# A decode attention and gated-MLP kernel: an eleventh load buffer, the output projection in pieces among the last V products, and a two-pass variance

## The chip, the cores and the metric

The kernel runs on one core of one Trainium2 chip. The metric is the device time of the program in microseconds, slower or faster by the median of its runs.

## The reference

Two branches read the same input `x` (4 tokens of 1024) and are mixed by a gate.

```python
g = sigmoid((x * gate_w).sum(-1, keepdims=True))
# branch A: attention of one new token over a cache, B=4, H=32, Sk=8192, Dh=128
q = x @ wq                                   # 1024 x 4096
p = softmax(q . k_cache * Dh**-0.5)          # k_cache, v_cache: 4 x 32 x 8192 x 128 bf16
a = (p @ v_cache).reshape(B, 1, 4096) @ wo   # 4096 x 1024
# branch B: gated MLP, F = 3584
z = gelu(x @ w_in); z1, z2 = halves of z
z2 = (z2 - mean) / sqrt(var + eps)
b = (z1 * (w_sp * z2 + b_sp)) @ w_out
out = g * a + (1 - g) * b
```

The caches are 2 x 128 tiles of 2 MB (one per token and head). With the weights the kernel reads 564.7 MB, and each byte of the cache is used once.

## The kernel before

All loads go through a ring of `NSLOT` slots of 2 MB, issued in one fixed order by SyncE. A load waits until its slot's last reader on TensorE is done.

```python
NSLOT = 10
LAG = 40                     # V of head t-40 is used at step t
...
BW_AT = [4 + (i * (LAG - 8)) // max(1, nbw) for i in range(nbw)]   # steps 4..30: 4 w_in, 2 w_out tiles
WO_AT = [NK + LAG - 18 + 2 * k for k in range(H // 8)]             # 4 w_o tiles, 18 V tiles before the end
for t in range(NK + LAG):    # the order of the loads
    # t == 0: 4 w_q tiles;  t < 128: one K tile;  BW_AT: one w_in/w_out tile
    # WO_AT: one w_o tile as eight DMAs of 256 KB;  t >= 40: one V tile
    ...
```

At step `t` TensorE transposes K tile `t` (64 matmuls against the identity, evacuated by VectorE and ScalarE), then computes the scores of tile `t-1` and so frees its slot, then the V product of tile `t-40`. The first w_in tile is not used before step 41:

```python
def task_zT(t):
    ...
    if not dma_planned(r) or t < LAG + 1 or t < item_step[r] + 2:
        return False
```

After the 32 heads of a token their scores go through a softmax. Scores of the next token wait for it (`exp_done`), because they use the same PSUM banks. In that time TensorE may transpose two more K tiles, but frees no slot.

The layer norm of branch B takes mean and mean of squares in one pass (one matmul with ones for both). The output projection comes last:

```python
# after the last V product
d_ot = event("dve")
plan("dve", lambda E: E.tensor_copy(OT_sb[:, 0:Bn * 32], PS[:, OT_OFF:OT_OFF + Bn * 32]), waits=[last_pv], ev=d_ot)
for qi, r in enumerate(wo_items):
    def fn_a(E, qi=qi, s=s):
        for hh in range(8):
            for c in range(NC_):          # 4 x 8 x 8 = 256 matmuls, 4 columns each
                ins = E.matmul(PS[:, AT_OFF + c * Bn:...], lhsT=ring[:, s, hh * DM + c * 128:...], rhs=otv[:, h, :], ...)
    plan("pe", fn_a, waits=waits, ev=p_a)
# then: diff, times gate, plus B; 8 transposes; copy; output DMA
```

Of the kernel before, what the change touches and what calls it, by code (L numbers as in the profile page):

```python
# [5 lines left out]
BF = mybir.dt.bfloat16  # L6
# [2 lines left out]
ALU = mybir.AluOpType  # L9
AX = mybir.AxisListType  # L10

NSLOT = 10
SLOT_COLS = 8192
LAG = 40
KT_BANKS = (4, 5, 7)
# [5 lines left out]
def bass_gated_mix__mha_block_cached__mixer_gmlp__decode_kernel(  # L21
# [41 lines left out]
    RMAXT_OFF = 3584  # L63
    GMB_OFF = 3712
    SUM_OFF = 3713
    XTB_OFF = 5 * 1024

    es = ExitStack()
    with es:
# [9 lines left out]
        Q4 = sbt("Q4", [128, 128], F32)  # L79
        onesF = sbt("onesF", [128, 128], F32)  # L80
        IrowB = sbt("IrowB", [128, 1024], BF)
        x_sb = sbt("x_sb", [128, DM], BF)
        gw_sb = sbt("gw_sb", [128, DM], BF)
        xT_sb = sbt("xT_sb", [128, NI * Bn], BF)
        Qm = sbt("Qm", [128, Bn * H * 32], BF)
        zwork = sbt("zwork", [128, 6, NZ], F32)
# [7 lines left out]
        E2_sb = sbt("E2_sb", [128, 2, 2048], BF)  # L94
        OT_sb = sbt("OT_sb", [128, 128], BF)
        out_sb = sbt("out_sb", [128, DM], BF)
        junk = sbt("junk", [128, DM], BF)
        sm = sbt("sm", [128, 16], F32)
        wspb = sbt("wspb", [128, 2], BF)
        gm_sb = sbt("gm_sb", [128, 160], F32)  # L100
# [110 lines left out]
        item_step = {}  # L211
        nbw = len(extra) - 4
        BW_AT = [4 + (i * (LAG - 8)) // max(1, nbw) for i in range(nbw)]
        WO_AT = [NK + LAG - 18 + 2 * k for k in range(H // 8)]
        for t in range(NK + LAG):
            if t == 0:
                for q in range(4):
# [165 lines left out]
        gel = zwork[:, 4, :]  # L383
        z2sq = zwork[:, 5, 0:NFH * Bn]
        gT = zwork[:, 1, 0:NFH * Bn]
        bstate = dict(z_next=0, z_done=None, d8=None, bt_done=False, ln_planned=False, d6=None, d6a=None)

        def task_zT(t):
            q = bstate["z_next"]
# [27 lines left out]
        def plan_bchain(z_done):  # L417
            d1 = event("dve")
            plan("dve", lambda E: E.tensor_copy(zz, PS[:, ZT_OFF:ZT_OFF + NZ]), waits=[z_done], ev=d1)
            add_reader(6, d1)  # L420
            d2 = event("dve")
            plan("dve", lambda E: E.tensor_tensor(zsq, zz, zz, ALU.mult), waits=[d1], ev=d2)
            d3 = event("dve")
            plan("dve", lambda E: E.tensor_scalar(zsq, zsq, 0.044715, 1.0, op0=ALU.mult, op1=ALU.add),
                 waits=[d2], ev=d3)
            d4 = event("dve")
            plan("dve", lambda E: E.tensor_tensor(targ, zsq, zz, ALU.mult), waits=[d3], ev=d4)
            a_sg = event("act")
            plan("act", lambda E: E.activation(sg, targ, ACTF.Sigmoid, scale=GELU_C2), waits=[d4], ev=a_sg)
            d5 = event("dve")  # L430
            plan("dve", lambda E: E.tensor_tensor(gel, zz, sg, ALU.mult), waits=[a_sg], ev=d5)
            z2v = gel[:, NFH * Bn:NFC * Bn]
            d6a = event("dve")
            plan("dve", lambda E: E.tensor_reduce(st[:, 0:Bn], z2v.rearrange("p (f b) -> p b f", b=Bn), AX.X, ALU.add),
                 waits=[d5], ev=d6a)
            d6b = event("dve")
            plan("dve", lambda E: E.tensor_tensor(z2sq, z2v, z2v, ALU.mult), waits=[d5], ev=d6b)
            d6 = event("dve")
            plan("dve", lambda E: E.tensor_reduce(st[:, Bn:2 * Bn], z2sq.rearrange("p (f b) -> p b f", b=Bn),
                                                  AX.X, ALU.add), waits=[d6b], ev=d6)  # L440
            bstate["d6"] = d6
            bstate["d6a"] = d6a
            bstate["d4"] = d4

        def task_LN(t):
            if bstate["ln_planned"] or bstate["d6"] is None:
                return False
            bstate["ln_planned"] = True
            p_ln = event("pe")
            plan("pe", lambda E: E.matmul(PS[:, LN_OFF:LN_OFF + 2 * Bn], lhsT=onesF[:, :], rhs=st[:, 0:2 * Bn],  # L450
                                          start=True, stop=True),
                 waits=[bstate["d6"], bstate["d6a"], g_ones] + readers(6), ev=p_ln)
            d7a = event("dve")
            plan("dve", lambda E: E.tensor_scalar(st[:, 8:8 + 2 * Bn], PS[:, LN_OFF:LN_OFF + 2 * Bn], 1.0 / FH, None,
                                                  op0=ALU.mult), waits=[p_ln], ev=d7a)
            add_reader(6, d7a)
            mean = st[:, 8:8 + Bn]
            ex2 = st[:, 8 + Bn:8 + 2 * Bn]
            d7b = event("dve")
            plan("dve", lambda E: E.tensor_tensor(st[:, 24:24 + Bn], mean, mean, ALU.mult), waits=[d7a], ev=d7b)  # L460
            d7 = event("dve")
            plan("dve", lambda E: E.tensor_tensor(st[:, 16:16 + Bn], ex2, st[:, 24:24 + Bn], ALU.subtract),
                 waits=[d7b], ev=d7)
            a_std = event("act")
            plan("act", lambda E: E.activation(st[:, 20:20 + Bn], st[:, 16:16 + Bn], ACTF.Sqrt, bias=sm[:, 7:8],  # L465
                                               scale=1.0), waits=[d7, g_sm], ev=a_std)
            d_rstd = event("dve")
            plan("dve", lambda E: E.reciprocal(st[:, 28:28 + Bn], st[:, 20:20 + Bn]), waits=[a_std], ev=d_rstd)
            z2v = gel[:, NFH * Bn:NFC * Bn]
            z2m = z2v.rearrange("p (f b) -> p f b", b=Bn)  # L470
            gTm = gT.rearrange("p (f b) -> p f b", b=Bn)
            dg = None
            for b in range(Bn):
                dg = event("dve")
                plan("dve", lambda E, b=b: E.tensor_scalar(gTm[:, :, b], z2m[:, :, b], st[:, 8 + b:9 + b],
                                                           st[:, 28 + b:29 + b], op0=ALU.subtract, op1=ALU.mult),
                     waits=[d_rstd, bstate["d4"]], ev=dg)
            dg2 = event("dve")
            plan("dve", lambda E: E.tensor_scalar(gT, gT, sm[:, 8:9], sm[:, 9:10], op0=ALU.mult, op1=ALU.add),
                 waits=[dg, d_wsp], ev=dg2)  # L480
            d8 = event("dve")
            z1v = gel[:, 0:NFH * Bn]
            plan("dve", lambda E: E.tensor_tensor(uT[:, :], z1v, gT, ALU.mult), waits=[dg2], ev=d8)
            bstate["d8"] = d8
            return True
# [114 lines left out]
        def softmax_stage(b):  # L600
# [29 lines left out]
            elif st_ == 1:  # L630
# [14 lines left out]
                e2_ready[b] = e5  # L645
                sm_state[b] = 2

        def plan_PV(b, h):
            nonlocal last_pv
            r = kv_items[("V", b, h)]  # L650
            wt = need(r)
            s = slot_of(r)
            pv_ev = event("pe")

            def fn_v(E, s=s, b=b, h=h):
                ins = None
                col = OT_OFF + b * 32 + h
                for j in range(JT):
                    ins = E.matmul(PS[:, col:col + 1], lhsT=ring[:, s, j * 128:(j + 1) * 128],  # L659
                                   rhs=E2_sb[:, b % 2, j * 32 + h:j * 32 + h + 1], start=(j == 0), stop=(j == JT - 1))  # L660
                return ins
            waits = [wt] + readers(6)
            if h == 0:
                waits += [e2_ready[b], qstate["qm_ready"]]
            plan("pe", fn_v, waits=waits, ev=pv_ev)
            consume(r, pv_ev)
            last_pv = pv_ev
            return pv_ev

        pendS = []  # L670
        pv_next = 0
        t = 0
        while pv_next < NK:
            newT = None
            if t == 0:
                task_QT(t)
# [29 lines left out]
        assert bstate["bt_done"]  # L706
        exp_done_last = exp_done[Bn - 1]

        d_ot = event("dve")
        plan("dve", lambda E: E.tensor_copy(OT_sb[:, 0:Bn * 32], PS[:, OT_OFF:OT_OFF + Bn * 32]), waits=[last_pv], ev=d_ot)  # L710
        add_reader(6, d_ot)
        otv = OT_sb[:, 0:Bn * 32].rearrange("p (b h) -> p h b", h=32)
        p_a = None
        for qi, r in enumerate(wo_items):
            wt = need(r)
            s = slot_of(r)
            p_a = event("pe")

            def fn_a(E, qi=qi, s=s):
                ins = None  # L720
                for hh in range(8):
                    h = qi * 8 + hh
                    for c in range(NC_):
                        ins = E.matmul(PS[:, AT_OFF + c * Bn:AT_OFF + (c + 1) * Bn],  # L724
                                       lhsT=ring[:, s, hh * DM + c * 128:hh * DM + (c + 1) * 128],
                                       rhs=otv[:, h, :],
                                       start=(h == 0 and c == 0), stop=(h == H - 1 and c == NC_ - 1))
                return ins
            waits = [wt]
            if qi == 0:  # L730
                waits += [d_ot] + readers(6)
            plan("pe", fn_a, waits=waits, ev=p_a)
        for r in wo_items:
            consume(r, p_a)
        assert next_dma == len(items)
# [2 lines left out]
        prod = fin[:, 1, 0:NCB]  # L738
        outT = fin[:, 2, 0:NCB]
        d_f1 = event("dve")  # L740
        plan("dve", lambda E: E.tensor_tensor(diff, PS[:, AT_OFF:AT_OFF + NCB], BT_sb[:, 0:NCB], ALU.subtract),
             waits=[p_a, bstate["d_bt"]], ev=d_f1)
        d_f2 = event("dve")
        plan("dve", lambda E: E.tensor_tensor(prod.rearrange("p (c b) -> p c b", b=Bn),
# [65 lines left out]
```

## Time and profile before

| | before |
|---|---|
| median of the runs | 1390.78 us (15 runs, 1388.83 to 1394.03) |
| span of the profiled run | 1386.9 us (a run of 1388.73 us) |
| HBM read | 564.7 MB |
| 2 MB tile in the V stage | every 4.90 us |
| start of the last V product to the end | 14.96 us |

From the page of the kernel before, the span in 40 slices of 34.7 us: DMA busy share in tenths, and the rate in GB/s.

```profile
DMA  9999997999999999999999999999999999998994
GB/s 353 420 419 420 416 417 306 383 417 427 424 424 426 425 425 427 426 424 426 425 425 425 427 426 425 426 426 425 425 426 426 423 428 425 425 380 352 414 427 183
```

The DMA engines are the limit: 9 tenths and about 425 GB/s in all but a few slices. The Trainium skill ("DMA: Bandwidth & Descriptors", Specifications) states a fabric ceiling of 435 GB/s, and the trace saturates 2% below it. So one reads this profile by its holes: the first slice, the slice of 306 (208 to 243 us), those of 380 and 352, and the last.

The end of the timeline (start us, duration us, engine, line of the kernel, operation; in brackets the idle time before it and what ended it). PE is TensorE and PEld its weight loads, DVE is VectorE, ACT ScalarE, POOL GpSimd, and SPq the queue of SyncE:

```profile
1371.94 1.86 PE L659 MATMUL PS<-E_sb,ring 128*128 128x1 bf16 x64 [3.00 <-DMA ring<-in_A_v_cache_dram]
1373.84 0.29 DVE L710 CAST OT_sb<-PS 128x128 bf16<-128x128 f32 x1 [207.64 <-PE PS L659]
...
1374.28 6.97 PE L724 MATMUL PS<-OT_sb,ring 128*128 128x4 bf16 x256 [0.48 <-DVE OT_sb L710]
1381.29 0.19 DVE L741 TENSOR_TENSOR fin<-PS,BT_sb 128x32 f32<-128x32 f32 x1 [7.15 <-PE PS L724]
...
1381.99 1.87 PE L755 MATMUL PS<-identF,fin 128*4 128x128 f32 x8 [0.74 <-DVE fin L749]
...
1385.13 0.29 SPq L761 DMA_DIRECT2D out_dram<-out_sb  x1
```

When the last V tile has landed, nothing is left to stream, and 15 us of dependent work follow, 7 us of them the projection.

The first softmax, in windows of 3 us (window, length, then busy time and instruction count of PE, PEld, DVE, ACT and POOL, then granted clock, DMA share and GB/s):

```profile
221.00:224.00 3.00, 3.00 (x42) 2.90 (x43) 1.97 (x4) 1.02 (x1) 0.00 (x0) 0.69 0.56 240
224.00:227.00 3.00, 3.00 (x70) 2.78 (x70) 1.65 (x3) 1.99 (x2) 0.00 (x0) 1.00 0.68 191
227.00:230.00 3.00, 3.00 (x70) 2.67 (x67) 2.35 (x5) 2.11 (x3) 0.00 (x0) 1.00 0.92 377
...
233.00:236.00 3.00, 1.89 (x31) 1.53 (x27) 2.06 (x4) 2.35 (x3) 0.00 (x0) 1.00 1.00 399
236.00:239.00 3.00, 2.38 (x40) 2.36 (x40) 1.86 (x5) 2.75 (x2) 0.00 (x0) 1.00 0.38 164
239.00:242.00 3.00, 1.86 (x31) 1.51 (x27) 1.86 (x4) 2.31 (x5) 0.00 (x0) 1.00 0.02 5
242.00:245.00 3.00, 2.11 (x66) 1.92 (x66) 1.83 (x4) 0.84 (x1) 0.00 (x0) 1.00 0.00 0
245.00:248.00 3.00, 2.78 (x54) 2.55 (x47) 3.00 (x4) 1.12 (x2) 0.00 (x0) 1.00 0.95 284
```

The last column falls to 240 and 191, recovers, and then goes to 164, 5 and 0. Lost stream is the sum of (425 - rate)/425 x 3 us: 3.3 us in 221-230, 8.8 us in 236-248, 12.1 us in all. This counts bytes; how much time it cost is seen in e5. SyncE's timeline, the loads issued there (from three narrow windows):

```profile
225.04 0.33 SPq L281 DMA_DIRECT2D ring<-in_A_k_cache_dram  x1
...
229.71 0.33 SPq L281 DMA_DIRECT2D ring<-in_A_k_cache_dram  x1
...
244.31 1.20 SPq L281 DMA_DIRECT2D ring<-in_A_k_cache_dram  x2
```

No load is issued for 14.6 us. TensorE starts no score group between 229.7 and 243.2 us, and of the ten slots six hold w_in and w_out tiles that nobody has used yet. By the completion events in the trace one load is outstanding at 230 us, and none at 242.

### The profile page before, as it was taken

How to read it: one execution, taken by the hardware profiler on the slowest of the kernel's cores; microseconds unless marked ns; L12 is line 12 of the kernel's file. 1: busy time of each engine (PE TensorE's matmuls, PEld its weight loads, DVE VectorE, ACT ScalarE, POOL GpSimd, SP SyncE). 2: the span in 40 equal slices, each digit the busy share in tenths (PEclk: the TensorE clock that was granted, in tenths of full speed). 3: DMA queues.
4: the chain of work that ended last, by engine and by line, in shares of the span. 5: the costliest groups of instructions: out<-in, count | busy, mean ns of one | idle time of the engine just before them, and what ended most of it. 6: DMA issues, size and time to landing. Idle time of an engine off the chain costs nothing.

```text
span 1386.9 us, 44335 instructions
## 1 busy us (share of the span) xinstructions
PE 1005.0 (72%) x21368; PEld 931.1 (67%) x21368; DVE 462.4 (33%) x702; ACT 408.4 (29%) x400; POOL 4.7 (0%) x21
## 2 busy tenths in 40 slices
PE   2888887888978787877788777878778875332235
PEld 2878876777877677777777777777777775332234
DVE  1556555624333234333333334323233332000000
ACT  0545555523323233322323233323232321000000
POOL 1000000000000000000000000000000000000000
PEclk9989999988888888888888889888888886555555
DMA  9999997999999999999999999999999999998994
GB/s 353 420 419 420 416 417 306 383 417 427 424 424 426 425 425 427 426 424 426 425 425 425 427 426 425 426 426 425 425 426 426 423 428 425 425 380 352 414 427 183
DMA packets 52107, 567.53 MB, mean 409 GB/s; under 512 B 5069, under 2 KB 6093, under 8 KB 19161
## 3 DMA queue, kind: packets, MB, share of 16 engines
q1 hardware_dynamic: 51928, 564.70, 97.0%
q8 instruction: 167, 2.74, 0.8%
q14 instruction: 12, 0.09, 0.0%
HBM read 564.68 MB, written 0.01 MB: 407 GB/s over the span
## 4 chain that ended last, share of the span: by engine, by line
DMA 76%; PE 19%; ACT 2%; issue 1%; SPq 1%; DVE 1%
DMA ring<-in_A_k_cache_dram 59%; DMA ring<-in_A_v_cache_dram 18%; PE PS L552 11%; PE PS L659 4%; PE PS L580 3%; ACT ring L565 2%; SPq L281 1%; PE PS L724 1%; PE PS L405 0%; PE PS L505 0%; DVE sm L595 0%; ACT E_sb L625 0%; PE PS L755 0%; SPq L171 0%; ACT L465 0%
## 5 line engine op out<-in xcount | busy, mean ns | idle before, releaser
L552 PE MATMUL PS<-identB,ring 128*128 128x128 bf16 x8192 | 626.4, 248 | 198.2 <-DMA ring<-in_A_k_cache_dram 178.4
L552 PEld LDWEIGHTS PS<-identB,ring 128*128 128x128 bf16 x8192 | 587.0, 114 | 231.6 <-issue 187.4
L563 DVE COPY ring<-PS 128x1024 bf16<-128x1024 bf16 x640 | 425.3, 689 | 651.8 <-PE PS L552 648.9
L565 ACT ACTIVATE ring<-PS 128x1024 bf16<-128x1024 bf16 x384 | 393.0, 1024 | 737.2 <-PE PS L552 737.2
L659 PE MATMUL PS<-E_sb,ring 128*128 128x1 bf16 x8192 | 230.5, 164 | 147.9 <-DMA ring<-in_A_v_cache_dram 143.1
L659 PEld LDWEIGHTS PS<-E_sb,ring 128*128 128x128 bf16 x8192 | 218.9, 98 | 170.5 <-DMA ring<-in_A_v_cache_dram 147.4
L580 PE MATMUL PS<-ring,Qm 128*32 128x256 bf16 x4096 | 136.0, 275 | 2.9 <-issue 2.8
L580 PEld LDWEIGHTS PS<-ring,Qm 128*32 128x32 bf16 x4096 | 98.1, 97 | 17.5 <-issue 3.4
L710 DVE CAST OT_sb<-PS 128x128 bf16<-128x128 f32 x1 | 0.3, 293 | 207.6 <-PE PS L659 207.6
L339 PE MATMUL PS<-xT_sb,ring 128*128 128x4 bf16 x256 | 7.5, 166 | 13.2 <-DMA ring<-in_A_wq_dram 13.2
L339 PEld LDWEIGHTS PS<-xT_sb,ring 128*128 128x128 bf16 x256 | 7.1, 104 | 13.5 <-DMA ring<-in_A_wq_dram 13.5
L352 DVE TENSOR_TENSOR Qm<-PS,IrowB 128x1024 bf16<-128x1024 f32 x4 | 4.6, 1218 | 20.4 <-PE PS L339 20.4
L595 DVE TENSOR_REDUCE sm<-PS 128x1 f32<-128x2048 f32 x4 | 9.2, 2292 | 6.3 <-PE PS L580 6.3
L625 ACT ACTIVATE E_sb<-PS,sm 128x2048 bf16<-128x2048 f32 x4 | 7.9, 1967 | 8.7 <-DVE sm L621 8.7
L643 DVE STREAM_TRANSPOSE E_sb<-E_sb 128x2048 bf16<-128x2048 bf16 x4 | 9.2, 2312 | 0.1
L724 PE MATMUL PS<-OT_sb,ring 128*128 128x4 bf16 x256 | 7.0, 168 | 0.5 <-DVE OT_sb L710 0.5
L724 PEld LDWEIGHTS PS<-OT_sb,ring 128*128 128x128 bf16 x256 | 6.9, 103 | 0.5 <-issue 0.5
L405 PE MATMUL PS<-xT_sb,ring 128*128 128x4 bf16 x224 | 6.2, 164 | 0.0
L405 PEld LDWEIGHTS PS<-xT_sb,ring 128*128 128x128 bf16 x224 | 6.1, 96 | 0.0
L618 PEld LDWEIGHTS PS<-sm,gm_sb 1*128 1x128 f32 x8 | 1.4, 213 | 3.4 <-DVE gm_sb L613 3.4
L312 PE MATMUL PS<-identB,x_sb 4*128 4x4 bf16 x8 | 0.4, 164 | 4.5 <-DMA wspb<-in_B_b_sp_dram 4.5
L618 PE MATMUL PS<-sm,gm_sb 1*128 1x1 f32 x8 | 1.7, 281 | 2.5 <-DVE gm_sb L613 2.5
(67 smaller groups left out, 42.9 us busy)
## 6 DMA issues: line engine op xcount, KB each, us to landing
ring<-in_A_k_cache_dram SPq DMA_DIRECT2D x128, 2048.0 KB, 40.8
ring<-in_A_v_cache_dram SPq DMA_DIRECT2D x128, 2048.0 KB, 38.3
ring<-in_A_wq_dram SPq DMA_DIRECT2D x4, 2048.0 KB, 16.1
ring<-in_A_wo_dram SPq DMA_DIRECT2D x32, 256.0 KB, 15.8
ring<-in_B_w_in_dram SPq DMA_DIRECT2D x3, 2048.0 KB, 36.1
ring<-in_B_w_out_dram SPq DMA_DIRECT2D x1, 2048.0 KB, 18.6
ring<-in_B_w_out_dram SPq DMA_DIRECT2D x1, 1536.0 KB, 12.1
ring<-in_B_w_in_dram SPq DMA_DIRECT2D x1, 1024.0 KB, 21.1
```

The costliest lines, as they stand in the source:

```text
L281: plan(it["eng"], lambda E, dst=dst, src=src: E.dma_start(dst, src), waits=waits, dma=(sem_slot[s], 16))
L339: ins = E.matmul(PS[:, QT_OFF + h * Bn:QT_OFF + (h + 1) * Bn], lhsT=ring[:, s_, i * 1024 + (h % 8) * 128:i * 1024 + (h % 8) * 128 + 128], ...
L405: ins = E.matmul(PS[:, ZT_OFF + fc * Bn:ZT_OFF + (fc + 1) * Bn], lhsT=ring[:, s, i * w + lc:i * w + lc + 128], rhs=xT_sb[:, i * Bn:(i + 1) ...
L552: ins = E.transpose(PSb[:, bank * 1024 + jj * 128:bank * 1024 + (jj + 1) * 128], ring[:, s, j * 128:(j + 1) * 128], identB[:, :])
L563: plan("dve", lambda E, dst=dst, src=src: E.tensor_copy(dst, src), waits=[pe_ev], ev=ev_e)
L565: plan("act", lambda E, dst=dst, src=src: E.activation(dst, src, ACTF.Copy), waits=[pe_ev], ev=ev_e)
L580: ins = E.matmul(PS[kq * 32:(kq + 1) * 32, g * 256:(g + 1) * 256], lhsT=lhsT, rhs=kt[:, :, kq * 32:(kq + 1) * 32], start=(h == 0 and g % 2 ...
L595: plan("dve", lambda E: E.tensor_reduce(sm[:, 0:1], PS[:, 0:SW], AX.X, ALU.max), waits=[sc_ev], ev=e1_)
L625: plan("act", lambda E: E.activation(E_sb[:, 0:SW], PS[:, 0:SW], ACTF.Exp, bias=sm[:, 1:2], scale=SCALE, accum_out=sm[:, 2:3]), waits=[e3, ...
L643: plan("dve", lambda E: E.transpose(E2_sb[:, b % 2, 0:SW], E_sb[:, 0:SW]), waits=[e4], ev=e5)
L659: ins = E.matmul(PS[:, col:col + 1], lhsT=ring[:, s, j * 128:(j + 1) * 128], rhs=E2_sb[:, b % 2, j * 32 + h:j * 32 + h + 1], start=(j == 0 ...
L724: ins = E.matmul(PS[:, AT_OFF + c * Bn:AT_OFF + (c + 1) * Bn], lhsT=ring[:, s, hh * DM + c * 128:hh * DM + (c + 1) * 128], rhs=otv[:, h, : ...
```

## The change

The intent is to shorten the end of the kernel by doing the projection while the last V tiles stream, and to give the ring one slot more. The two-pass variance is presumably for accuracy. The core of the diff:

```diff
-NSLOT = 10
+NSLOT = 11
...
-        junk = sbt("junk", [128, DM], BF)
+        junk = out_sb                       # the slot's room: x, gate weights and junk
+            x_sb = E_sb[:, 0:DM]            # share memory that is used later
+            gw_sb = E_sb[:, DM:2 * DM]
...
-        WO_AT = [NK + LAG - 18 + 2 * k for k in range(H // 8)]
+        WO_AT = [NK + LAG - 24 + 2 * k for k in range(H // 8)]
...
+        def plan_A_heads(upto):             # heads lo..upto
+            plan("dve", copy of O's columns lo..upto to OT_sb, waits=[last_pv])
+            plan("pe", 8 matmuls per head into PSUM bank 7, waits=[copy, all four w_o tiles])
+            n_wide = (17 if upto >= 23 else 5) if upto - lo == 2 else 0
+            # n_wide matmuls identB x IrowB[:, 0:512] into banks 4, 5; nobody reads them
...
         def plan_PV(b, h):
             ...
+            if wo_ok and b == Bn - 1:       # from head 16 of the last token on
+                plan_A_heads(min(h, astate["n_done"] + 2))
...
-        # 256 matmuls after the last V product
+        plan_A_heads(H - 1)                 # nothing is left to do here
```

The layer norm's part replaces the mean of squares by subtracting the mean first, squaring, reducing, and a second small matmul; four normalizing steps become one.

(The lines of `plan_A_heads` are abridged to their sense. Heads 0 to 23 come in eight groups of three after the V products of heads 16 to 23, with 7 x 5 + 17 = 52 matmuls that only fill time; heads 24 to 31 singly.)

More of the change, by code (lines that the diff above doesn't have):

```diff
@@ L65, in bass_gated_mix__mha_block_cached__mixer_gmlp__decode_kernel @@
     SUM_OFF = 3713
+    AT7_OFF = 3840
     XTB_OFF = 5 * 1024
@@ L81, in bass_gated_mix__mha_block_cached__mixer_gmlp__decode_kernel @@
         IrowB = sbt("IrowB", [128, 1024], BF)
-        x_sb = sbt("x_sb", [128, DM], BF)
-        gw_sb = sbt("gw_sb", [128, DM], BF)
         xT_sb = sbt("xT_sb", [128, NI * Bn], BF)
@@ L96, in bass_gated_mix__mha_block_cached__mixer_gmlp__decode_kernel @@
         out_sb = sbt("out_sb", [128, DM], BF)
-        junk = sbt("junk", [128, DM], BF)
+        junk = out_sb
+        if 2 * DM <= 2048:
+            x_sb = E_sb[:, 0:DM]
+            gw_sb = E_sb[:, DM:2 * DM]
+        else:
+            x_sb = sbt("x_sb", [128, DM], BF)
+            gw_sb = sbt("gw_sb", [128, DM], BF)
         sm = sbt("sm", [128, 16], F32)
@@ L385, in bass_gated_mix__mha_block_cached__mixer_gmlp__decode_kernel @@
         gT = zwork[:, 1, 0:NFH * Bn]
-        bstate = dict(z_next=0, z_done=None, d8=None, bt_done=False, ln_planned=False, d6=None, d6a=None)
+        bstate = dict(z_next=0, z_done=None, d8=None, bt_done=False, ln_planned=False, d6=None)
         def task_zT(t):
@@ L432, in plan_bchain @@
             z2v = gel[:, NFH * Bn:NFC * Bn]
-            d6a = event("dve")
+            d6 = event("dve")
             plan("dve", lambda E: E.tensor_reduce(st[:, 0:Bn], z2v.rearrange("p (f b) -> p b f", b=Bn), AX.X, ALU.add),
-                 waits=[d5], ev=d6a)
-            d6b = event("dve")
-            plan("dve", lambda E: E.tensor_tensor(z2sq, z2v, z2v, ALU.mult), waits=[d5], ev=d6b)
-            d6 = event("dve")
-            plan("dve", lambda E: E.tensor_reduce(st[:, Bn:2 * Bn], z2sq.rearrange("p (f b) -> p b f", b=Bn),
-                                                  AX.X, ALU.add), waits=[d6b], ev=d6)
+                 waits=[d5], ev=d6)
             bstate["d6"] = d6
-            bstate["d6a"] = d6a
             bstate["d4"] = d4
@@ L448, in task_LN @@
             bstate["ln_planned"] = True
+            z2v = gel[:, NFH * Bn:NFC * Bn]
+            z2m = z2v.rearrange("p (f b) -> p f b", b=Bn)
+            gTm = gT.rearrange("p (f b) -> p f b", b=Bn)
             p_ln = event("pe")
-            plan("pe", lambda E: E.matmul(PS[:, LN_OFF:LN_OFF + 2 * Bn], lhsT=onesF[:, :], rhs=st[:, 0:2 * Bn],
+            plan("pe", lambda E: E.matmul(PS[:, LN_OFF:LN_OFF + Bn], lhsT=onesF[:, :], rhs=st[:, 0:Bn],
                                           start=True, stop=True),
-                 waits=[bstate["d6"], bstate["d6a"], g_ones] + readers(6), ev=p_ln)
+                 waits=[bstate["d6"], g_ones] + readers(6), ev=p_ln)
             d7a = event("dve")
-            plan("dve", lambda E: E.tensor_scalar(st[:, 8:8 + 2 * Bn], PS[:, LN_OFF:LN_OFF + 2 * Bn], 1.0 / FH, None,
+            plan("dve", lambda E: E.tensor_scalar(st[:, 8:8 + Bn], PS[:, LN_OFF:LN_OFF + Bn], 1.0 / FH, None,
                                                   op0=ALU.mult), waits=[p_ln], ev=d7a)
@@ L457, in task_LN @@
             mean = st[:, 8:8 + Bn]
-            ex2 = st[:, 8 + Bn:8 + 2 * Bn]
             d7b = event("dve")
-            plan("dve", lambda E: E.tensor_tensor(st[:, 24:24 + Bn], mean, mean, ALU.mult), waits=[d7a], ev=d7b)
+            plan("dve", lambda E: E.tensor_tensor(gTm, z2m, mean.unsqueeze(1).broadcast_to([128, NFH, Bn]),
+                                                  ALU.subtract), waits=[d7a, bstate["d4"]], ev=d7b)
+            d7c = event("dve")
+            plan("dve", lambda E: E.tensor_tensor(z2sq, gT, gT, ALU.mult), waits=[d7b], ev=d7c)
+            d7d = event("dve")
+            plan("dve", lambda E: E.tensor_reduce(st[:, Bn:2 * Bn], z2sq.rearrange("p (f b) -> p b f", b=Bn),
+                                                  AX.X, ALU.add), waits=[d7c], ev=d7d)
+            p_ln2 = event("pe")
+            plan("pe", lambda E: E.matmul(PS[:, LN_OFF + Bn:LN_OFF + 2 * Bn], lhsT=onesF[:, :], rhs=st[:, Bn:2 * Bn],
+                                          start=True, stop=True), waits=[d7d] + readers(6), ev=p_ln2)
             d7 = event("dve")
-            plan("dve", lambda E: E.tensor_tensor(st[:, 16:16 + Bn], ex2, st[:, 24:24 + Bn], ALU.subtract),
-                 waits=[d7b], ev=d7)
+            plan("dve", lambda E: E.tensor_scalar(st[:, 16:16 + Bn], PS[:, LN_OFF + Bn:LN_OFF + 2 * Bn], 1.0 / FH, None,
+                                                  op0=ALU.mult), waits=[p_ln2], ev=d7)
+            add_reader(6, d7)
             a_std = event("act")
@@ L468, in task_LN @@
             plan("dve", lambda E: E.reciprocal(st[:, 28:28 + Bn], st[:, 20:20 + Bn]), waits=[a_std], ev=d_rstd)
-            z2v = gel[:, NFH * Bn:NFC * Bn]
-            z2m = z2v.rearrange("p (f b) -> p f b", b=Bn)
-            gTm = gT.rearrange("p (f b) -> p f b", b=Bn)
-            dg = None
-            for b in range(Bn):
-                dg = event("dve")
-                plan("dve", lambda E, b=b: E.tensor_scalar(gTm[:, :, b], z2m[:, :, b], st[:, 8 + b:9 + b],
-                                                           st[:, 28 + b:29 + b], op0=ALU.subtract, op1=ALU.mult),
-                     waits=[d_rstd, bstate["d4"]], ev=dg)
+            dg = event("dve")
+            plan("dve", lambda E: E.tensor_tensor(gTm, gTm, st[:, 28:28 + Bn].unsqueeze(1).broadcast_to([128, NFH, Bn]),
+                                                  ALU.mult), waits=[d_rstd], ev=dg)
             dg2 = event("dve")
@@ L646, in softmax_stage, with fn_ac, fn_wide @@
                 sm_state[b] = 2
+        astate = dict(started=False, n_done=0, total=Bn * H, last_ev=None, ot_copied=0)
+        def plan_A_heads(upto):
+            lo = astate["n_done"]
+            if upto < lo:
+                return
+            d_otc = event("dve")
+            otv = OT_sb[:, 0:Bn * 32].rearrange("p (b h) -> p b h", h=32)
+            psv = PS[:, OT_OFF:OT_OFF + Bn * 32].rearrange("p (b h) -> p b h", h=32)
+            plan("dve", lambda E, lo=lo, upto=upto: E.tensor_copy(otv[:, :, lo:upto + 1], psv[:, :, lo:upto + 1]),
+                 waits=[last_pv], ev=d_otc)
+            add_reader(6, d_otc)
+            pa = event("pe")
+            oth = OT_sb[:, 0:Bn * 32].rearrange("p (b h) -> p h b", h=32)
+            def fn_ac(E, lo=lo, upto=upto):
+                ins = None
+                for h_ in range(lo, upto + 1):
+                    s_ = slot_of(wo_items[h_ // 8])
+                    hh = h_ % 8
+                    for c in range(NC_):
+                        ins = E.matmul(PS[:, AT7_OFF + c * Bn:AT7_OFF + (c + 1) * Bn],
+                                       lhsT=ring[:, s_, hh * DM + c * 128:hh * DM + (c + 1) * 128],
+                                       rhs=oth[:, h_, :],
+                                       start=(h_ == 0 and c == 0), stop=(h_ == H - 1 and c == NC_ - 1))
+                return ins
+            plan("pe", fn_ac, waits=[d_otc] + [need(r) for r in wo_items] + readers(7), ev=pa)
+            n_wide = (17 if upto >= 23 else 5) if upto - lo == 2 else 0
+            def fn_wide(E, n_wide=n_wide):
+                ins = None
+                for k in range(n_wide):
+                    ins = E.matmul(PS[:, (4 + k % 2) * 512:(5 + k % 2) * 512], lhsT=identB[:, :],
+                                   rhs=IrowB[:, 0:512], start=True, stop=True)
+                return ins
+            if n_wide:
+                plan("pe", fn_wide, waits=readers(4) + readers(5))
+            astate["n_done"] = upto + 1
+            astate["last_ev"] = pa
         def plan_PV(b, h):
@@ L667, in plan_PV @@
             last_pv = pv_ev
+            idx = b * H + h
+            wo_ok = (all(dma_planned(rr) for rr in wo_items) and cur_step[0] >= WO_AT[-1] + 2
+                     and len(sm_state) == Bn and all(v == 2 for v in sm_state.values()))
+            if wo_ok and b == Bn - 1:
+                plan_A_heads(min(h, astate["n_done"] + 2))
             return pv_ev
@@ L672, in bass_gated_mix__mha_block_cached__mixer_gmlp__decode_kernel @@
         t = 0
+        cur_step = [0]
         while pv_next < NK:
+            cur_step[0] = t
             newT = None
@@ L707, in bass_gated_mix__mha_block_cached__mixer_gmlp__decode_kernel @@
         exp_done_last = exp_done[Bn - 1]
-        d_ot = event("dve")
-        plan("dve", lambda E: E.tensor_copy(OT_sb[:, 0:Bn * 32], PS[:, OT_OFF:OT_OFF + Bn * 32]), waits=[last_pv], ev=d_ot)
-        add_reader(6, d_ot)
-        otv = OT_sb[:, 0:Bn * 32].rearrange("p (b h) -> p h b", h=32)
-        p_a = None
-        for qi, r in enumerate(wo_items):
-            wt = need(r)
-            s = slot_of(r)
-            p_a = event("pe")
-            def fn_a(E, qi=qi, s=s):
-                ins = None
-                for hh in range(8):
-                    h = qi * 8 + hh
-                    for c in range(NC_):
-                        ins = E.matmul(PS[:, AT_OFF + c * Bn:AT_OFF + (c + 1) * Bn],
-                                       lhsT=ring[:, s, hh * DM + c * 128:hh * DM + (c + 1) * 128],
-                                       rhs=otv[:, h, :],
-                                       start=(h == 0 and c == 0), stop=(h == H - 1 and c == NC_ - 1))
-                return ins
-            waits = [wt]
-            if qi == 0:
-                waits += [d_ot] + readers(6)
-            plan("pe", fn_a, waits=waits, ev=p_a)
+        plan_A_heads(H - 1)
+        assert astate["n_done"] == H
+        p_a = astate["last_ev"]
         for r in wo_items:
@@ L740, in bass_gated_mix__mha_block_cached__mixer_gmlp__decode_kernel @@
         d_f1 = event("dve")
-        plan("dve", lambda E: E.tensor_tensor(diff, PS[:, AT_OFF:AT_OFF + NCB], BT_sb[:, 0:NCB], ALU.subtract),
+        plan("dve", lambda E: E.tensor_tensor(diff, PS[:, AT7_OFF:AT7_OFF + NCB], BT_sb[:, 0:NCB], ALU.subtract),
              waits=[p_a, bstate["d_bt"]], ev=d_f1)
```

## The prediction

> **What bounds the kernel now.** The stream of tiles from HBM. The activity slices show DMA at 9 tenths nearly everywhere, about 425 GB/s. The Trainium skill ("DMA: Bandwidth & Descriptors", Specifications) gives a fabric ceiling of 435 GB/s; the trace saturates close to it. In the V stage the timeline shows one 2 MB tile every 4.90 us with 1.87 us of TensorE work. 564.7 MB at that rate is 1319 us (estimate); the span is 1386.9. Time can be saved only where the stream stands still:
> 1. Tail. The last V product starts at 1371.94; then the cast of all O (0.29 us), 256 projection matmuls (6.97), three VectorE steps, transposes (1.87), copy (1.21), output DMA: 15 us.
> 2. First softmax. A table of 3 us windows shows 240 and 191 GB/s at 221-227 us and 164, 5, 0 at 236-245: about 12 us of streaming lost. Six of ten slots then hold w_in/w_out tiles for later, so four carry K. TensorE completes no score group between 229.7 and 243.2 us, no slot comes free, the next load is issued at 244.3.
> 3. A dip at 1240-1260 us (248, 243 GB/s), where w_o is issued as 32 small DMAs. V products keep their 4.9 us rhythm through it: nearly free.
>
> **What the change does.**
> - The projection is cut into head groups (8 of three heads, 8 of one) in TensorE's 3 us holes between the last V products; 15 small casts are added. After the last V one cast (0.2 us) and 8 matmuls (6.97/32 = 0.22 us) remain. End of last V product to first final subtraction: 7.5 us before, about 0.75 after. **-6.7 us, all critical.**
> - An eleventh slot (paid by aliasing x, gate weights and junk): five K slots instead of four in the first softmax, one tile more in the queue: **-4.9 us**, once. Elsewhere DMA is saturated: 0.
> - w_o six tiles earlier, so that it has landed for the first head group; seven slots remain for V. The dip moves along: 0.
> - 52 dummy 512-column matmuls, 0.43 us each at half clock (estimate from the skill, "TensorE: Matmul & The Clock Gate", 427 ns cold at N=512; no run here shows one yet). Five per group make a step of 1.9+0.5+0.7+2.1 = 5.2 us cold, less if the clock rises; the seventeen after head 23 set TensorE back about 5 us, which the remaining eight tiles (2.6 us of work each) absorb: 0. They don't warm the tail: 39 us of light work follow.
> - Two-pass variance: a second small matmul behind four VectorE steps stalls TensorE some 1.5 us once, near 333 us, where DMA is full: 0.
>
> **Prediction:** 1390.8 - 6.7 - 4.9 = about **1379 us**, 8 in 10 between **1373.5 and 1384.5**. Faster by over 2% 0.01, within 2% 0.98, slower by over 2% 0.01.
>
> **What would show it.** End of the timeline: 8.3 us from last V start to span end instead of 15. The 3 us table: the empty stretch at 236-245 shrinks to about 4 us, that at 221-227 fills. Chain of waits: the projection's 0.5% gone. V rhythm still 4.9 us through the head groups.
>
> **What would make it wrong.** Dummy matmuls or cast round trips delay slot release until the queue runs dry (V intervals above 4.9 us near the end). The eleventh slot saves nothing because the queue accepts no more transfers (with about 9 tiles in flight an issue already takes 3-4 us in the V stage), or saves more than a tile by preventing both gaps. A V wait starved by the earlier w_o.

## The result

| | before | after |
|---|---|---|
| median | 1390.78 us (15 runs) | 1376.78 us (8 runs, 1376.37 to 1378.44) |
| ratio | | 0.990 (95%: 0.9891 to 0.991) |
| span of the profiled run | 1386.9 | 1374.9 |
| start of the last V product | 1371.94 | 1366.72 |
| from there to the end | 14.96 | 8.18 |

A ratio is the mean time of one kernel's runs over that of the other's of the same rounds, so not quite the ratio of the medians.

The profiled span is 12.0 us shorter: 6.8 us of it at the end (14.96 - 8.18), and 5.2 us because the last V tile comes earlier (1371.94 - 1366.72). The medians differ by 14.0 us. The other 2 us are taken up below. The page of the changed kernel, the same lines:

```profile
DMA  9999999899999999999999999999999999979996
GB/s 352 421 417 421 418 416 389 370 425 425 424 425 426 425 425 427 426 425 426 425 427 425 426 425 426 426 425 425 427 424 426 425 426 425 421 312 408 427 425 253
```

The slice with the first softmax has risen from 306 to 389 GB/s. The dip of the w_o loads is still there, earlier (312 in slice 36). The end of the timeline:

```profile
1366.72 1.87 PE L703 MATMUL PS<-E_sb,ring 128*128 128x1 bf16 x64 [2.35 <-DMA ring<-in_A_v_cache_dram]
1368.62 0.17 DVE L661 CAST OT_sb<-PS 128x4 bf16<-128x4 f32 x1 [4.69 <-PE PS L703]
...
1368.86 0.38 PE L673 MATMUL PS<-OT_sb,ring 128*128 128x4 bf16 x8 [0.27 <-DVE OT_sb L661]
1369.27 0.19 DVE L771 TENSOR_TENSOR fin<-PS,BT_sb 128x32 f32<-128x32 f32 x1 [0.47 <-PE PS L673]
...
1369.97 1.87 PE L785 MATMUL PS<-identF,fin 128*4 128x128 f32 x8 [0.74 <-DVE fin L779]
...
1373.11 0.29 SPq L791 DMA_DIRECT2D out_dram<-out_sb  x1
```

The cast and the projection of one head are all that stands between the last V product and the subtraction. The windows of 3 us:

```profile
221.00:224.00 3.00, 3.00 (x61) 2.88 (x62) 2.35 (x4) 1.49 (x2) 0.00 (x0) 0.86 1.02 437
224.00:227.00 3.00, 3.00 (x66) 2.79 (x55) 1.72 (x3) 1.72 (x3) 0.00 (x0) 1.00 0.99 388
227.00:230.00 3.00, 3.00 (x70) 2.67 (x68) 2.34 (x4) 1.91 (x2) 0.00 (x0) 1.00 1.02 429
...
233.00:236.00 3.00, 1.38 (x21) 1.02 (x18) 1.98 (x5) 2.67 (x3) 0.00 (x0) 1.00 0.95 388
236.00:239.00 3.00, 2.72 (x42) 2.53 (x42) 1.94 (x5) 2.75 (x4) 0.00 (x0) 1.00 0.65 279
239.00:242.00 3.00, 1.51 (x24) 1.34 (x24) 1.55 (x3) 2.31 (x3) 0.00 (x0) 1.00 0.28 115
242.00:245.00 3.00, 2.62 (x74) 2.37 (x75) 2.13 (x3) 0.33 (x1) 0.00 (x0) 1.00 0.38 71
245.00:248.00 3.00, 2.78 (x51) 2.61 (x48) 3.00 (x5) 1.63 (x2) 0.00 (x0) 1.00 0.74 279
```

The hole at 221-227 is filled. That at 236-248 is smaller, 6.8 us of stream (before 8.8).

### The profile page after: what moved, and what is told of

Same layout as the page of the kernel before. It is cut to its first block, busy times and chain, and to the rows that moved or that the text cites. A ratio compares the mean times of both kernels' runs of the same rounds, so it can differ in the third digit from the quotient of the medians.

```text
span 1374.9 us, 44448 instructions
## 1 busy us (share of the span) xinstructions
PE 1028.3 (75%) x21414; PEld 941.9 (69%) x21422; DVE 464.4 (34%) x714; ACT 408.4 (30%) x400; POOL 4.7 (0%) x21
## 4 chain that ended last, share of the span: by engine, by line
DMA 76%; PE 17%; SPq 2%; ACT 2%; issue 1%; DVE 1%
DMA ring<-in_A_k_cache_dram 63%; DMA ring<-in_A_v_cache_dram 13%; PE PS L557 10%; PE PS L703 2%; PE PS L585 2%; ACT ring L570 2%; SPq L286 2%; PE PS L684 1%; SPq L276 1%; PE PS L673 0%; PE PS L410 0%; PE PS L510 0%; DVE E_sb L648 0%; DVE sm L600 0%; ACT E_sb L630 0%
## 5 line engine op out<-in xcount | busy, mean ns | idle before, releaser
L661 DVE CAST OT_sb<-PS 128x12 bf16<-128x12 f32 (+1 forms) x16 | 2.8, 177 | 204.9 <-PE PS L703 204.9
L684 PE MATMUL PS<-IrowB,identB 128*128 128x512 bf16 x44 | 19.6, 610 | 1.9 <-issue 1.9
L344 PEld LDWEIGHTS PS<-xT_sb,ring 128*128 128x128 bf16 x256 | 7.1, 104 | 13.5 <-DMA ring<-in_A_wq_dram 13.5
L684 PEld LDWEIGHTS PS<-IrowB,identB 128*128 128x128 bf16 x52 | 6.3, 133 | 9.6 <-issue 9.4
## 6 DMA issues: line engine op xcount, KB each, us to landing
ring<-in_B_w_in_dram SPq DMA_DIRECT2D x3, 2048.0 KB, 35.9
```

What stands on the lines that cost most here:

```text
L344: ins = E.matmul(PS[:, QT_OFF + h * Bn:QT_OFF + (h + 1) * Bn], lhsT=ring[:, s_, i * 1024 + (h % 8) * 128:i * 1024 + (h % 8) * 128 + 128], ...
L684: ins = E.matmul(PS[:, (4 + k % 2) * 512:(5 + k % 2) * 512], lhsT=identB[:, :], rhs=IrowB[:, 0:512], start=True, stop=True)
```

## The experiments

Twelve experiments ran, all correct; two of them are the kernel before, unchanged. Each batch had its own runs of the kernel before, with medians of 1391.5, 1390.7 and 1391.6 us.

### Each part alone

**e1_slot_only**: the kernel before with `NSLOT = 11` and the shared memory, nothing else.

> The kernel before with the eleventh slot (and the aliasing that pays for it) alone. Theory 1 (two separate savings: tail 6.8 us, and one tile of extra buffer in the first softmax 5.2 us): 1390.8 - 5.2 = 1385.5 us, ratio 0.996; last V product starts near 1366.7 as in the changed kernel, 15 us from there to the end as in the kernel before; the gap at 221-227 us filled, a gap at 236-247 us left. Rival A (the slot does nothing by itself, the earlier last tile comes from the earlier w_o or the head groups): 1390.8 us, ratio 1.000. Rival B (the slot also helps in the V stage): ratio below 0.994.

Measured: 1383.53 us, ratio 0.9943 (0.9928 to 0.9958). The last V product starts at 1367.12 us in the profile, and 15 us follow:

```profile
1367.12 1.87 PE L659 MATMUL PS<-E_sb,ring 128*128 128x1 bf16 x64 [4.42 <-DMA ring<-in_A_v_cache_dram]
```

So the earlier stream is the slot's work, and rival A is out. The ratio lies at the bound set for rival B (0.994), so e1 alone doesn't exclude it; e6 and e9 below do. At the median the slot gives about 8 us, more than the 5.2 expected; its profile, 4.8 us shorter than the profile of before, shows the expected size. Its windows have the hole at 221-227 us filled (426 and 366 GB/s) and the later one left (328, 147, 0 and 279 GB/s at 236-248).

**e2_tail_only**: the changed kernel with `NSLOT = 10`.

> The changed kernel with ten slots instead of eleven. Theory 1: 1390.8 - 6.8 = 1384.0 us, ratio 0.995; last V product starts near 1372 as before, 8.2 us from there to the end; the first softmax empties the DMA queue exactly as in the kernel before. Rival A: last V start near 1367, ratio 0.991. Rival C (with six V slots left, the dummy matmuls starve the queue): V intervals above 5 us in the head groups, ratio above 0.996.

Measured: 1385.54 us, ratio 0.9956 (0.9942 to 0.9971), 8.2 us from the last V product to the end, and the empty queue in the first softmax as before (169, 5, 0 GB/s at 236-245 us). Its profiled run, 1386.13 us, was one of the longer ones of its set, with the last V product at 1376.0 instead of about 1372, which is the same surplus as in e1 seen from the other side:

```profile
1376.02 1.87 PE L703 MATMUL PS<-E_sb,ring 128*128 128x1 bf16 x64 [2.35 <-DMA ring<-in_A_v_cache_dram]
```

V products start every 4.9 us in the head groups, and again at the end, so rival C is out. About 8 and 6 us add up to the 14 us measured.

### Where the surplus comes from

**e10_before_again_a** and **e11_before_again_b**: the kernel before, unchanged, two more profiles.

> The kernel before, unchanged, for a second profile. Its runs spread over 7 us (1388.5 to 1395.8) while the kernels without K shortage spread over 0.6 and 1.1 us, and the slot alone gained 8.0 us at the median although its profile shows only 4.8 us less than the profile of before (a run of 1388.7 us, among its fastest). Theory J (the rest of the gain is a loss of variable size while the queue refills after the first softmax): a run slower than 1388.7 us shows the extra time between the first and the last score groups of the K stage or before it, DMA rate below 416 GB/s at 250-300 us, and the same 15 us tail. Rival K (noise spread over the whole run): the extra time grows evenly over 300 to 1370 us.

> The same once more: theory J and rival K as in the run before it.

Measured: 1388.55 and 1391.69 us (one run each, state unknown). The last V product starts at 1371.67 and at 1374.90 us, 3.2 us apart, and the tails are alike. Windows of 3 us, first of the faster run, then of the slower:

```profile
290.00:293.00 3.00, 2.06 (x75) 1.73 (x64) 0.00 (x0) 0.00 (x0) 0.00 (x0) 1.00 0.97 366
293.00:296.00 3.00, 2.92 (x34) 2.95 (x35) 1.38 (x2) 1.02 (x1) 0.00 (x0) 0.63 1.01 426
```

```profile
290.00:293.00 3.00, 2.81 (x98) 2.78 (x101) 0.85 (x2) 1.16 (x2) 0.00 (x0) 1.00 0.67 279
293.00:296.00 3.00, 2.24 (x82) 1.94 (x71) 0.00 (x0) 0.00 (x0) 0.00 (x0) 0.89 0.89 279
```

The slower run has a third hole: 279 GB/s over 6 us, 2.1 us of stream. Between the two loads around it SyncE issued nothing for 10.9 us (281.55 to 292.43), in the faster run for 9.0 us. Another 1.2 us went at 240-250 us (134 against 184 GB/s). Counted over all bytes that the two traces had moved by then, at 425 GB/s, the slower run is level at 240 us, 1.2 us behind at 250, 1.3 at 290, 3.0 at 310 and 2.9 at 1100: after the refill nothing is added. The slow profile of e2 has the same hole (300 and 360 GB/s); the profile of the changed kernel, with eleven slots, has none (426 and 426). Theory J holds in the profiles at hand, rival K doesn't: with ten slots the queue can run dry a third time, by a size that differs from run to run, and the eleventh slot covers it. Four profiles show this; in how many runs it happens was not counted.

### What held the slots

**e5_late_weights_10**: the kernel before (ten slots) with the w_in and w_out loads moved behind the first softmax.

```diff
-        BW_AT = [4 + (i * (LAG - 8)) // max(1, nbw) for i in range(nbw)]
+        BW_AT = [LAG - 1 + 2 * i for i in range(nbw)]
```

> The kernel before (ten slots) with the w_in and w_out loads moved from steps 4 to 36 to steps 39 to 49, so that they hold no slot during the first softmax. Theory 1 (the queue ran dry there because six of ten slots were held by weights for later): both gaps vanish, DMA at about 425 GB/s from 200 to 260 us; 12 us less, 1378.5 us, ratio 0.991; tail still 15 us. Rival G (the gap is set by the 14 us in which TensorE completes no score group, whoever holds the slots): gap of 8 us stays, ratio above 0.996. Rival H (K tiles alone need TensorE 4.7 us each, so without weight tiles between them TensorE falls behind the stream and the time comes back as a new wait): between.

Measured: 1378.56 us (1378.28 to 1378.83), ratio 0.991 (0.9894 to 0.9926). (The loads stood at steps 4 to 30 before, not to 36 as the expectation has it.) Without weight tiles among them the K tiles come sooner, so the first softmax now falls earlier: TensorE starts no score group between 198.8 and 212.3 us. Windows of 3 us from that pause:

```profile
203.00:206.00 3.00, 1.27 (x17) 0.90 (x13) 1.65 (x4) 2.67 (x3) 0.00 (x0) 1.00 1.00 421
206.00:209.00 3.00, 2.45 (x41) 2.26 (x41) 2.14 (x4) 2.75 (x4) 0.00 (x0) 1.00 1.01 431
209.00:212.00 3.00, 1.52 (x25) 1.35 (x25) 1.29 (x2) 2.25 (x3) 0.00 (x0) 1.00 1.00 426
```

421, 431 and 426 GB/s where the kernel before had 164, 5 and 0. TensorE's pause is as long as ever, 13.5 us, but now the queue has loads for it: by the completion events eight are outstanding when the pause begins and five when it ends, against one and none in the kernel before. So the pause alone is no cost (rival G); the slots held for later use made it one. No new wait of rival H's kind is seen: counted in completed K and V tiles this run is 10.9 us ahead of the profile of before at the 60th tile, and 10.4 us at the last.

So the two holes cost about 10.4 us in time and not the 12.1 of the table, presumably because the table averages 16 DMA engines, while a tile is complete with its slowest (see e4). That the medians lie 12.1 us apart, just as expected, is in part luck: a run of before at the median (e11) has the third hole on top. One moved line is worth as much as the slot and the hidden projection without their last 2 us.

**e6_late_weights_11**: the changed kernel with the same line. **e9_late_weights_tail_10**: the same, with ten slots.

> The changed kernel with the same late weights. Theory 1: no gap is left for the eleventh slot to shorten, so it adds the tail's 6.8 us to the run with ten slots and late weights and nothing else: 1390.8 - 12.1 - 6.8 = 1372 us, ratio 0.986. Rival B (the slot helps elsewhere too): another 2 us or more below that.

> The changed kernel with late weights and only ten slots. Theory 1 (the eleventh slot is worth something only while weights hold six slots): the same as with eleven slots and late weights, 1372.0 us, ratio 0.986, within 1 us. Rival B (the slot helps in the V stage, where w_o holds four slots): slower by 2 us or more, and V intervals above 4.9 us there.

Measured: 1371.97 us (ratio 0.9862, 0.9846 to 0.9878) and 1371.84 us (ratio 0.9858, 0.9845 to 0.9872). With late weights the eleventh slot adds nothing, and the tail adds 6.6 us (1378.56 - 1371.97). Rival B is out, also for the stage in which w_o holds four slots. These two are the fastest kernels, 5 us below the changed kernel, and the second needs none of the shared memory.

### The parts that should be free

**e3_no_dummies**: the changed kernel with `n_wide = 0`.

> The changed kernel without its 52 dummy matmuls. Theory 1 (they fill time in which TensorE would wait for a tile): same as the changed kernel, 1376.8 us, within 0.5 us; V rhythm 4.90 us with TensorE waiting about 2.4 us for each tile. Rival D (they are a cost that the chain of waits names, about 42 us of it lies on them): faster by more than 1.5 us. Rival E (they keep the clock up for the end): slower by 1 us or more, tail above 8.2 us.

Measured: 1377.76 us, ratio 0.9899 (0.9883 to 0.9915); the changed kernel's 0.990 lies inside, though the median is 1.0 us above that of the other batch and not within the 0.5 expected. The tail is 8.2 us, so the dummies do nothing for the end either (rival E). The chain of waits of the changed kernel (start, duration, what) would make one expect more:

```profile
1295.03 1.91 PE PS L684 x4
1296.95 1.70 PE PS L703 x64
```

It runs through the dummy matmuls (L684) for 42 us. The timeline of one step, first of the changed kernel, then without the dummies, shows why they cost nothing (of five dummies four have a record):

```profile
1311.49 1.89 PE L703 MATMUL PS<-E_sb,ring 128*128 128x1 bf16 x64
...
1313.65 0.80 PE L673 MATMUL PS<-OT_sb,ring 128*128 128x4 bf16 x24 [0.27 <-DVE OT_sb L661]
...
1314.69 1.91 PE L684 MATMUL PS<-IrowB,identB 128*128 128x512 bf16 x4 [0.24 <-issue]
...
1316.40 1.89 PE L703 MATMUL PS<-E_sb,ring 128*128 128x1 bf16 x64
```

```profile
1311.21 1.87 PE L703 MATMUL PS<-E_sb,ring 128*128 128x1 bf16 x64 [1.95 <-DMA ring<-in_A_v_cache_dram]
1313.36 0.81 PE L673 MATMUL PS<-OT_sb,ring 128*128 128x4 bf16 x24 [0.27 <-DVE OT_sb L661]
1316.11 1.87 PE L703 MATMUL PS<-E_sb,ring 128*128 128x1 bf16 x64 [1.95 <-DMA ring<-in_A_v_cache_dram]
```

With them the step is 4.91 us (1311.49 to 1316.40), without them 4.90 us (1311.21 to 1316.11), with 1.95 us spent waiting for the V tile. The dummies fill that wait nearly to the last tenth. A chain takes whatever ended last; where two causes end within 0.1 us it says nothing about what taking one away is worth.

**e8_double_dummies**: twice as many.

> The changed kernel with twice the dummy matmuls (10 per group, 34 after head 23). Measured in the changed kernel: 0.43 us each at clock 0.50, a step of 4.91 us with five. If the clock stays at 0.50: steps of about 7 us, 2.1 us late per group, 7 groups 15 us, plus 34 x 0.43 = 14.6 us at the last; the remaining eight tiles regain about 2.4 us each: TensorE ends about 10 us late, 1387 us (theory 1: dummies are free only up to the idle 2.1 us per tile). If the clock rises to 1.00 under the denser load: dummies of 0.21 us, absorbed, 1377 us.

Measured: 1379.57 us, ratio 0.9914 (0.9899 to 0.9928), 2.8 us over the changed kernel: between the two cases expected. The clock neither stayed at 0.50 nor rose to 1.00 (windows of 10 us show 0.61, 0.73, 0.75, 0.59, 0.50 and 0.72 from 1290 to 1350 us), so steps took 5.8 to 7.0 us and TensorE ended 3 us late. So the dummies are free up to the wait they fill, and not beyond.

**e7_one_pass_ln**: the changed kernel with the old layer norm.

> The changed kernel with the one-pass variance of the kernel before. Theory 1 (TensorE's extra stall falls where the DMA queue is full): same as the changed kernel, within 0.5 us. Rival I (the stall of about 1.5 us shows): faster by 1 to 2 us.

Measured: 1376.62 us, ratio 0.9899 (0.9883 to 0.9915), the same. In the changed kernel the second small matmul waits 1.04 us for VectorE near 328 us, while DMA runs at 434 GB/s (320 to 330 us).

**e4_wo_one_dma**: each w_o tile as one DMA of 2 MB instead of eight of 256 KB. The edit, abridged:

```diff
-add_item("wo", [A_wo[(h0 + hh) * 128:(h0 + hh + 1) * 128, :] for hh in range(8)], 8 * DM, nparts=8)
+add_item("wout", A_wo[h0 * 128:(h0 + 8) * 128, :].rearrange("(hh p) n -> p hh n", p=128), 8 * DM)
```

> The changed kernel with each w_o tile loaded by one DMA of 2 MB instead of eight of 256 KB. The prediction held the dip at 1240-1260 us (1200-1230 in the changed kernel) for nearly free. Theory 1: within 1.5 us of the changed kernel (1376.8), though the dip disappears from the windows. Rival F (the dip is lost streaming; 282, 239 and 359 GB/s over 30 us against 425 is about 9 us of stream, worked out from the table): faster by 5 to 9 us, near 1369.

Measured: 1378.34 us, ratio 0.9903 (0.9888 to 0.9919), the same as the changed kernel. But the dip did not disappear. Windows of 10 us, first of the changed kernel, then with one DMA per tile:

```profile
1200.00:1210.00 10.00, 3.73 (x128) 3.57 (x128) 0.00 (x0) 0.00 (x0) 0.00 (x0) 0.50 0.69 282
1210.00:1220.00 10.00, 3.73 (x128) 3.57 (x129) 0.00 (x0) 0.00 (x0) 0.00 (x0) 0.50 0.59 239
```

```profile
1200.00:1210.00 10.00, 3.74 (x128) 3.58 (x128) 0.00 (x0) 0.00 (x0) 0.00 (x0) 0.50 0.84 341
1210.00:1220.00 10.00, 3.74 (x128) 3.57 (x128) 0.00 (x0) 0.00 (x0) 0.00 (x0) 0.50 0.50 213
```

So the number of DMAs doesn't make the dip, though the prediction put it down to the small DMAs. And since the dip stayed, the time of this run can't decide whether it costs anything (rival F). The completions of the tiles can. Counted in tiles of 2 MB (eight pieces of w_o as one), the kernel before completes one every 5.02 us in the mean at 700-1150 us and every 5.05 us at 1180-1310, through the dip (most follow after 4.9 us, a few later); in the changed kernel it is 5.01 and 5.02 us. So the dip is nearly free: 25 tiles at 0.03 us more are under 1 us.

What the dip is can be seen in the trace's completion events: each load has sixteen, one per DMA engine. The distance from the first to the last of them, averaged over the loads completed in a stretch of the kernel before, grows from 1.9 us at 250-300 us to 12.4 us at 700-750 and 23.3 us at 1150-1200. Some engines run far ahead of the slowest. When the w_o loads come, SyncE's issuing nearly stops; the eight pieces of the first tile take 38 us in the kernel before:

```profile
1217.85 38.32 SPq L271 DMA_DIRECT2D ring<-in_A_wo_dram  x8
```

With one DMA per tile the load behind the first w_o tile takes as long (35.9 us, from 1184.1). The leaders then run dry, while V products still start about every 4.9 us (the kernel before has them at 1240.49, 1245.46, 1250.33, 1255.59 and 1260.48), because a tile is complete when its slowest engine is done. Past the dip the distance is about 6 us. The rate falls, and the stream that the kernel waits for hardly does. That the leaders are the engines which run dry is inferred from these events; the trace as kept doesn't name the engines. Why the issuing stops at the w_o loads, and why some engines are slower, stays open.

**e12_wo_late**: the changed kernel with w_o at its old place.

```diff
-        WO_AT = [NK + LAG - 24 + 2 * k for k in range(H // 8)]
+        WO_AT = [NK + LAG - 18 + 2 * k for k in range(H // 8)]
```

> The changed kernel with the w_o loads where the kernel before had them (18 steps before the end instead of 24). Head groups then start at head 22 instead of 16: ten groups of three, two heads left for the end. Theory 1: two heads instead of one after the last V product, plus dummy matmuls that now run to the end (5 or 17 in each group of three, 17 from head 23 on: 7 us in 4.9 us steps): TensorE falls behind by about 5 us per group in the last groups, so slower than the changed kernel by tens of us, near 1400. Without that (if the clock rises to 1.00 and the dummies take 0.21 us each): within 3 us of 1376.8. Rival A (earlier w_o is worth nothing in itself) holds in either case if the V rhythm before the first head group stays 4.9 us.

Measured: 1386.84 us, ratio 0.9968 (0.9952 to 0.9983). The size was missed both ways. Three groups with 17 dummies now come at the very end and take 6.3, 5.2 and 3.6 us by the records, the clock rising to 0.93 meanwhile; the last V product starts at 1373.27. The DMA has fallen to 87 GB/s in 1360-1370 us, as in the changed kernel (102), so the stream itself was not late. So the earlier w_o keeps the head groups and their dummies away from the end. No run moves it alone, so that it has no worth beyond this is not shown; the 6.6 us of e6 against e5 leave no room for one. How much of the 10 us is the dummies' alone was not tried.

## Why the prediction was right

It said 1379 us (1373.5 to 1384.5); measured were 1376.8.

- *Tail, -6.7 us.* Shown: 14.96 to 8.18 us in the profiles, -6.8; e2 (-6.0 at the median) and e6 against e5 (-6.6) show it without the slot's gain.
- *Eleventh slot, -4.9 us, once.* The mechanism is right (e1, e5, e9), the size somewhat low. Between the two profiles it is 5.2 us; the table of windows gives 12.1 - 6.8 = 5.3. In the median run it is 8 us by e1; the slower profiles with ten slots (e11, e2) have a third hole at 290-296 us that the faster ones lack. The prediction was worked out from one profile, and that run (1388.73 us) was one of the fastest of its kernel. This is the term that was mis-sized, and its 3 us (8 against 4.9) are enough for the 2 us between prediction and result. Whether most runs have this hole was not counted; it is seen in these profiles.
- *The stretch at 236-245 shrinks to about 4 us and that at 221-227 fills.* The second is right. The first lost 6.8 us of stream instead of 4: the extra tile was spent on the earlier hole.
- *Elsewhere the slot gives nothing.* Right (e9).
- *Dummies 0.* Right in the time (e3). In the detail the step came out as 4.91 us, not 5.2, and the clock did not rise in the steps of five.
- *Two-pass variance 0.* Right (e7); the stall was 1.04 us, not 1.5.
- *The dip is nearly free.* Right, by the rhythm of the completed tiles; its reason, 32 small DMAs, was wrong (e4).

## What to carry to other kernels

In a kernel that streams at the limit, read the stream's holes and ask which buffers are taken at that moment: loading weights behind the pause instead of up to 37 steps ahead of their use (e5) was worth more than one buffer more. Work that hangs behind the last tile goes into the waits ahead of it. And before a size is taken from one profile, compare that run with the spread of the others.

## What the Trainium skill lacked or had wrong

- "TensorE: Matmul & The Clock Gate" (Part 1: The HAM clock gate) says that the clock rises after one window of about 3.4 us of sustained activity, but not how full a window must be. Here TensorE was busy 8.97 of 10 us in steps of 4.91 us, and the granted clock stayed at 0.50; with twice the dummies (9.2 to 9.4 of 10 us) it was 0.50 to 0.75. Its cold figure of 426.7 ns for 512 columns agrees: 427 ns from start to start of the dummies' weight loads (six steps from 1329.44 to 1332.00 us).
- "DMA: Bandwidth & Descriptors" (Why a DMA increments its semaphore by 16 and not by 1) says that the engines of one DMA finish independently. It has no size for it: here the sixteen completions of a 2 MB load lay 23 us apart in the mean at 1150-1200 us, with eight to ten loads in the queue.
- The same page (Issuing engines are not separate DMA queues) calls the sequencer's issue time usually small. It has nothing on a full queue: an issue that took 0.33 us elsewhere took 4.2 us again and again, and once 13.3 us, while ten to six DMAs were outstanding, nine of them loads of 2 MB at first (1217 to 1256 us in the kernel before).
- The same page (Specifications) lists 358 GB/s as the HBM limit of one core. This run on one core held 425 GB/s from HBM, as the page's own measurement on a core alone does; the page gives 358 as the part of each when both cores of a pair stream, and the row is right only with that note.
- No page has the pattern: buffers held for later use drain a queue during a pause of the consumer. Here that cost 12.1 us of stream and 10.4 us of time (e5 and before, profiles).
